# Attention units of one head pair over all batches, first outputs moved inside SBUF, one mask pass for both score banks, and four short decay scans in place of one long one

## The chip, the cores and the metric

The kernel runs on one core of one Trainium2 chip. The metric is the device time of one execution in microseconds (us), lower is better. The engines are called here by the names of the trace: PE (TensorE, matmuls), PEld (its weight loads), DVE (VectorE), ACT (ScalarE), POOL (GpSimd) and SP (SyncE, which issues the DMAs; SPq, ACTq and so on are the instruction queues of the engines). SBUF is the core's working memory with 128 partitions, PSUM the banks that matmuls write, DRAM the device memory.

## The reference, cut to what matters

```python
# attention with decay: q, k, v, alpha are [B=4, H=8, S=768, D=48]
for t in range(S):
    state = alpha[:, :, t, :, None] * state + einsum('bhd,bhe->bhde', k[:, :, t], v[:, :, t])
    y[:, :, t] = einsum('bhd,bhde->bhe', q[:, :, t], state)
x = y.transpose(0, 2, 1, 3).reshape(3072, 384)          # token by (head, d)
# layer 1
h = x @ w_in                                            # 384 -> 2048
g = (a0 + a1*h + a2*h**2 + a3*h**3) / (1 + |b0|*|h| + |b1|*h**2 + 1e-6)
x = g @ w_out                                           # 2048 -> 384
# layer 2
h = x @ w_in2;  out = (h * cos(h)) @ w_out2
```

The attention is computed in chunks. Inside a chunk of 128 steps, p is the running product of alpha; q is multiplied by p and k by 1/p, the scores are a causal matrix product of the two, and the state is carried from chunk to chunk with the last p of the chunk (`pc`).

## The kernel before, in words

The sequence is cut into 6 chunks of 128 steps. A **unit** of the attention is one chunk of one batch: 4 head pairs side by side on the columns (4 x 128 = 512), the two heads of a pair on the partitions. There are 24 units, and unit u stands for chunk u // 4, batch u % 4. The order of the work is written out by hand: a loop over slots n = -3 to 24, in each of which `attention(n)` issues one step for several units at once, and then the fetches and the conversion of the layers' weights. From slot 20 on (`LEAD`) layer 1 begins beside the last four units. After that PE works through layer 1 and layer 2 in blocks of 512 tokens (NF = 16 tiles of 128 hidden columns each), the last blocks with a three-by-three fast product ("threes").

What one regular slot of the attention asks of each engine:

- DVE: `decay` (a 128x4 max, L259, which seeds the first column, and one running product of 512 columns, L260, whose second operand `fresh` is a PSUM bank that holds a floor value everywhere else); `last_decay` (L268); the two steps of the reciprocal (L284, L292); two steps of weight conversion (L75, L76); two of the state's update (L355, L357). In slots 2 to 6 also `y_lo` (L406).
- POOL: q times p (`scale_q`, L303) and k times 1/p (`scale_k`, L298), the low half of a weight (L205), and `mask1`, the causal selection, once for each of the two score banks (L323, tiles hi and lo, 512 columns each).
- ACT: `mask0`, the copy of each score bank out of PSUM (L318, twice), Ln and Exp for 1/p (L275, L276), the output's and the transposed k's copy (L400, L336), and three steps of weight conversion (L70, L71, L195).
- PE: `scores` (L311), the state's part and the scores' part of the output (L376, L386), the transposes (L331) and the update (L343).
- SP: loads of a (the decays), kq and v for later units, one weight tile, and the store of a finished output (`y_store`, L416). Outputs are kept in two buffers in turn, so `y_out` of unit u waits until the store of unit u - 2 has landed.

Layer 1 reads its input x with head features on the partitions and 512 tokens on the columns. The first block's input (chunk 0) is wanted as a high and a low half. Before, the outputs of the first four units go to DRAM as two halves (`y_store`, with `rest=True` for the low one) and come back as 8 loads of rows of 128 floats (`x_pieces`, L1307, slots 8 to 15). The later blocks' inputs are read back by `x_load`, 4 DMAs each (L675). All DMAs go through SP's queue in the order written; a DMA also waits until the one eight before it has landed. An instruction of SP that waits holds up all behind it.

The score banks are the PSUM tiles acc0 and acc1, which the layers use for their sums too. The weight conversion has one PSUM bank (`words_t`) for its intermediate words.

Of the kernel before, what the change touches and what calls it, by code (L numbers as in the profile page):

```python
# [40 lines left out]
def attn_then_two_moe(ctx, tc, kqT, aT, vP, w1i, w1o, ma, mb, w2i, w2o, out):  # L41
# [6 lines left out]
    x0d = dram.tile([2, B, 128 * HP, C], F32, name="x0")  # L48
# [10 lines left out]
    def to_f32(t, r, by=None):  # L59
# [9 lines left out]
        def words():  # L69
# [6 lines left out]
            lambda: nc.vector.scalar_tensor_tensor(ti, hi, -0x80000000, both, ALU.bitwise_and, ALU.bitwise_or),  # L76
# [17 lines left out]
    def temp(tag, dtype=F32, shape=(128, TB)):  # L94

        bufs = {"z": 3, "ah": 2, "g": 4, "hi": 3, "lo": 3}[tag]
        return el.tile(list(shape), dtype, tag=tag, name=tag, bufs=bufs)
# [6 lines left out]
    fresh = bank("r1", (128, HP, C))  # L104
    words_t = bank("b2", (128, TB), I32)[:, :DM]
# [4 lines left out]
    a_t = [a_all[:, i] for i in range(3)]  # L110
# [5 lines left out]
    ws = [[wp.tile([128, 2, DM], F32R, tag=f"w{s}_{i}", name=f"w{s}_{i}") for i in range(NF)] for s in range(2)]  # L116
# [12 lines left out]
    y_rest = xt[0, 0].rearrange("p a b c -> p (a b c)")  # L129
# [3 lines left out]
    MORE = 20  # L133
    slot = [0]
# [25 lines left out]
    def words_bank(w):  # L160

        if slot[0] <= LEAD + 2 and not later[0]:
            return words_t
# [4 lines left out]
    def tick(k, ahead=0):  # L168

        while k and steps and (len(steps) > ahead or fetched[0] == fetched[1]):  # L170
            w, i = steps[0]
            if i == 0:
                t = st_all[:, w_order.index(w) % 4]
                stage[w] = t, to_f32(t, raw64.pop(w), words_bank(w))
# [23 lines left out]
    def w_lo(engs):  # L198
        engs = list(engs)
        while to_lo:  # L200
            (m, s, i), hi = to_lo.pop(0)
# [3 lines left out]
            engs[0].tensor_tensor(out=lo, in0=full, in1=hi.bitcast(F32), op=ALU.subtract)  # L205
            engs.append(engs.pop(0))
# [16 lines left out]
    def load(u, name):  # L223
# [9 lines left out]
        elif u == 0 and name == "a":  # L233
            for cs in (slice(0, HP + HP // 2 * C), slice(HP + HP // 2 * C, HP * (C + 1))):
                nc.sync.dma_start(out=t[:, cs], in_=src[:, cs])
# [17 lines left out]
    def decay(u):  # L253
# [3 lines left out]
        first, rest = a[:, :HP].unsqueeze(2), a[:, HP:].rearrange("p (a b) -> p a b", a=HP)  # L257
        for hs in parts(u):
            nc.vector.tensor_tensor(out=fresh[:, hs, 0:1], in0=first[:, hs], in1=fresh[:, hs, 1:2], op=ALU.max)  # L259
            nc.vector.tensor_tensor_scan(  # L260
                d["p"][:, hs].rearrange("p a b -> p (a b)"), rest[:, hs].rearrange("p a b -> p (a b)"),
                fresh[:, hs].rearrange("p a b -> p (a b)"), 0.0, ALU.mult, ALU.max,
            )

    def last_decay(u):
        d = U[u]
        d["pc"] = in_p.tile([128, HP, 1], F32, tag="pc", name="pc", bufs=6)
        nc.vector.tensor_tensor(out=d["pc"], in0=d["p"][:, :, C - 1:], in1=fresh[:, :, 1:2], op=ALU.max)  # L268
# [36 lines left out]
    def scores(u):  # L305
        d = U[u]
        d["sc"] = [ps_acc.tile([128, HP, C], F32, tag=f"acc{j}", name=f"sc{j}") for j in range(2)]
# [5 lines left out]
    def mask0(u):  # L313
        d = U[u]
        d["s"] = []
        for j, sc in enumerate(d.pop("sc")):
            s = temp(("hi", "lo")[j], shape=(128, HP, C))
            nc.scalar.activation(out=s, in_=sc, func=AF.Copy, scale=-1.0)  # L318
            d["s"].append(s)
# [41 lines left out]
    def y_state(u):  # L361
        c, b = divmod(u, B)
        d = U[u]
        if u == NU - 1:
            d["y"] = ps_acc.tile([128, HP, C], F32, tag="acc0", name="y")
# [25 lines left out]
    def y_out(u):  # L391
        d = U[u]
        if u < NU - B:
            d["yo"] = kept[2 + u % 2]
            if 2 <= u < B:
                d["yo"] = y_rest[:, (2 + u) * TB:(3 + u) * TB].bitcast(F32).rearrange("p (a t) -> p a t", a=HP)
# [1110 lines left out]
```

## Time and profile before

| what | value |
|---|---|
| time, median of 3 runs | 918.09 us (916.93 to 919.14) |
| the profiled execution's own time | 916.58 us |
| its span in the trace | 914.9 us |
| PE busy | 893.7 us, 98% of the span |
| DVE, ACT, POOL busy | 703.8, 695.5, 710.0 us |
| granted TensorE clock | 1.00 in every window that was read |

The times of the rows further down are microseconds from the start of the span of the profiled execution. Its own time is 1.68 us longer than the span, and 1.51 us below the median of the runs.

### The profile page before, as it was taken

The page shows a single profiled execution, that of the slowest core. Times are in us where ns is not written, and L with a number is a line of the kernel's source. Part 1 is how long each engine was busy: PE and PEld are TensorE (multiplying, and loading weights), DVE is VectorE, ACT ScalarE, POOL GpSimd, SP SyncE. Part 2 cuts the span into 40 slices and gives each one's busy share as a digit, 9 for nine tenths or more (in the row PEclk, how much of TensorE's full clock was granted, in tenths as well). Part 3 has the DMA queues.
Part 4 walks back from the last instruction along what each step waited for, and adds up shares of the span by engine and source line. Part 5 has one row for each costly group of instructions (what it writes and reads, how often), then busy time and mean ns, then how long its engine had stood idle before and what let it go on. Part 6 is the DMA issues. An engine that isn't in the chain of part 4 may idle for free.

```text
span 914.9 us, 15676 instructions
## 1 busy us (share of the span) xinstructions
PE 893.7 (98%) x5348; PEld 740.6 (81%) x5348; DVE 703.8 (77%) x1247; ACT 695.5 (76%) x1302; POOL 710.0 (78%) x699
## 2 busy tenths in 40 slices
PE   7899989999999999999999999999999999999997
PEld 6787767888888888888888888878888888888885
DVE  8998789999899989979979968666367554555552
ACT  6998888888879788878778878756577666666653
POOL 7999999989789979879879767758887475655332
PEclk9999999999999999999999999999999999999999
DMA  9999840100234132232165467530243432533432
GB/s 324 388 380 379 331 132 18 31 22 18 69 113 121 44 126 74 78 121 87 41 190 195 153 209 252 196 120 27 69 139 104 155 123 89 171 104 104 139 104 90
DMA packets 67305, 128.83 MB, mean 141 GB/s; under 512 B 6928, under 2 KB 30224, under 8 KB 67216
## 3 DMA queue, kind: packets, MB, share of 16 engines
q1 hardware_dynamic: 67216, 127.74, 41.4%
q8 instruction: 44, 0.72, 0.3%
q14 instruction: 45, 0.37, 0.1%
HBM read 95.21 MB, written 32.51 MB: 140 GB/s over the span
## 4 chain that ended last, share of the span: by engine, by line
PE 86%; ACT 6%; DMA 3%; DVE 3%; issue 2%; POOL 0%; SPq 0%; ACTq 0%; DVEq 0%
PE b L537 28%; PE acc L553 28%; PE acc L1032 15%; PE b L997 6%; PE r L997 5%; DMA x0d<-g 1%; PE b L1176 1%; ACT hi L318 1%; ACT lo L318 1%; ACT r L275 1%; ACT st L70 1%; DMA kq<-kqT 1%; ACT g L336 1%; ACT w L195 1%; DVE p L260 1%
## 5 line engine op out<-in xcount | busy, mean ns | idle before, releaser
L537 PE MATMUL b<-x,w 128*128 128x512 f32 x1143 | 288.2, 396 | 2.5 <-DVE g L606 1.4
L537 PEld LDWEIGHTS b<-x,w 128*128 128x128 f32 x1143 | 214.3, 188 | 55.4 <-DVE g L606 2.0
L553 PE MATMUL acc<-hi,w 128*128 128x512 f32 x738 | 251.5, 395 | 0.0
L588 POOL TENSOR_TENSOR lo<-g,hi 128x512 fp32r<-128x512 f32 x128 | 173.5, 1355 | 70.0 <-ACT hi L583 63.7
L553 PEld LDWEIGHTS acc<-hi,w 128*128 128x128 f32 x738 | 138.7, 188 | 32.9
L1089 POOL TENSOR_TENSOR lo<-g,hi 128x512 fp32r<-128x512 f32 x64 | 83.0, 1297 | 103.6 <-ACT hi L1088 91.6
L553 PE MATMUL acc<-lo,w 128*128 128x512 f32 x369 | 146.2, 396 | 0.0
L583 ACT ACTIVATE hi<-g 128x512 fp32r<-128x512 f32 x128 | 80.6, 630 | 80.7 <-DVE g L619 43.4
L614 POOL TENSOR_TENSOR z<-z,ah 128x512 f32<-128x512 f32 x96 | 127.2, 1325 | 8.0
L1032 PE MATMUL acc<-hi,w_out 128*128 128x512 f32 x384 | 130.4, 396 | 0.0
L615 DVE TENSOR_TENSOR g<-g,b 128x512 f32<-128x512 f32 x96 | 65.3, 680 | 24.0 <-ACT g L612 23.4
L553 PEld LDWEIGHTS acc<-lo,w 128*128 128x128 f32 x369 | 69.4, 188 | 17.0
L1032 PEld LDWEIGHTS acc<-hi,w_out 128*128 128x128 f32 x384 | 68.7, 188 | 9.9
L1032 PE MATMUL acc<-lo,w_out 128*128 128x512 f32 x192 | 76.3, 397 | 0.4 <-POOL lo L1089 0.2
L613 POOL TENSOR_SCALAR z<-ah,cq 128x512 f32<-128x512 f32 x96 | 74.7, 778 | 2.1 <-ACT ah L611 2.1
L612 ACT ACTIVATE g<-b,cq 128x512 f32<-128x512 f32 x96 | 74.5, 776 | 0.0
L619 DVE SCALAR_TENSOR_TENSOR g<-g,cq,r 128x512 f32<-128x512 f32 x96 | 70.8, 738 | 0.1
L606 DVE SCALAR_TENSOR_TENSOR g<-g,cq,b 128x512 f32<-128x512 f32 x96 | 70.7, 736 | 0.0
L623 ACT ACTIVATE r<-z,lnb 128x512 f32<-128x512 f32 x96 | 66.7, 695 | 1.1 <-POOL z L614 1.1
L608 DVE SCALAR_TENSOR_TENSOR r<-z,r 128x512 f32<-128x512 f32 x96 | 65.6, 683 | 0.0
L603 DVE SCALAR_TENSOR_TENSOR z<-z,r 128x512 f32<-128x512 f32 x96 | 64.9, 676 | 0.0
L611 ACT ACTIVATE ah<-b 128x512 f32<-128x512 f32 x96 | 56.4, 587 | 7.5 <-PE b L537 7.3
(192 smaller groups left out, 1814.9 us busy)
## 6 DMA issues: line engine op xcount, KB each, us to landing
w_out<-wd SPq DMA_DIRECT2D x64, 384.0 KB, 3.0
kq<-kqT SPq DMA_DIRECT2D x24, 512.0 KB, 6.5
raw<-w2i SPq DMA_DIRECT2D x16, 384.0 KB, 3.5
w<-wd SPq DMA_DIRECT2D x16, 384.0 KB, 3.0
raw<-w2o SPq DMA_DIRECT2D x16, 384.0 KB, 3.3
wd<-w SPq DMA_DIRECT2D x16, 384.0 KB, 2.5
a<-aT SPq DMA_DIRECT2D x23, 258.0 KB, 5.7
v<-vP SPq DMA_DIRECT2D x24, 192.0 KB, 6.4
```

The source lines that it names most:

```text
L537: nc.tensor.matmul(h, ws[0][f][:, w, ks], x[:, xx, kk, :], start=i == 0, stop=i == 8)
L553: nc.tensor.matmul(acc[k], ws[1][f][:, w, ks], d[g], start=first and i == 0, stop=last and i == 2)
L583: nc.scalar.activation(out=t["hi"], in_=t["g"], func=AF.Copy)
L588: eng.tensor_tensor(out=t["lo"], in0=t["g"], in1=t["hi"].bitcast(F32), op=ALU.subtract)
L606: nc.vector.scalar_tensor_tensor(g, g, cq[:, 3:4], two["h"], ALU.add, ALU.mult)
L612: nc.scalar.activation(out=g, in_=h, func=AF.Identity, scale=cq[:, 5:6], bias=cq[:, 4:5])
L613: nc.gpsimd.tensor_scalar(zz, ah, cq[:, 1:2], cq[:, 0:1], ALU.mult, ALU.add)
L614: nc.gpsimd.tensor_tensor(out=zz, in0=zz, in1=ah, op=ALU.mult)
L619: nc.vector.scalar_tensor_tensor(g, g, cq[:, 2:3], r, ALU.add, ALU.mult)
L997: nc.tensor.matmul(tile[:, half], w[p], x[q], start=start and i == 0, stop=True, skip_group_check=True)
L1032: nc.tensor.matmul(acc[k], item["w"][:, w, ks], item[g], start=first, stop=last)
L1089: nc.gpsimd.tensor_tensor(out=p["lo"], in0=p["g"], in1=p["hi"].bitcast(F32), op=ALU.subtract)
```

## The change

A unit becomes one chunk of one head pair over all four batches: the host lays the inputs out so, and the columns of a unit are 4 batches x 128 steps. The work on the engines for one unit keeps its shape. The input `a` loses its four extra columns (258 KB becomes 256 KB a load). With it:

- The first four units' outputs stay in SBUF (`y_home`, which is the space of the last eight of the layer's first weights) and are moved from there to layer 1's input by 10 DMAs inside SBUF (`y_move`, L437, slots 3 to 6), with both halves in one DMA. The 8 stores and 8 loads of before fall away.
- `x_load` of later blocks makes 10 DMAs of 48, 32 or 16 rows of 2 KB (L690) where 4 DMAs with rows of 512 bytes stood.
- acc0 and acc1 become the halves of one PSUM tile `pair`; `mask0` is one copy of 1024 columns (L328), `mask1` one selection of 1024 columns (L333).
- `decay` is four running products of 128 columns, each of which starts from 1.0 (L272); the floor is one PSUM column, broadcast. There is no max ahead of them.
- The words of the weight conversion go to two banks in turn, and the floor's column is read from the bank that is not in use.

```diff
+    words_t = [bank(tag) for tag in ("b2", "r1")]
+    def floor(shape):
+        t = words_t[1 - lately[0]][:, DM:DM + 1]
+        return (t if len(shape) == 2 else t.unsqueeze(1)).to_broadcast(shape)
+    pair = ps_acc.tile([128, 2, TB], F32, tag="acc01", name="acc01")
+    w_late = wp.tile([128, 2 * B, 2, DM], F32R, tag="w0_8", name="w0_8")
+    y_home = w_late.rearrange("p i a b -> p i (a b)")
...
-        for hs in parts(u):
-            nc.vector.tensor_tensor(out=fresh[:, hs, 0:1], in0=first[:, hs], in1=fresh[:, hs, 1:2], op=ALU.max)
+        for h in range(HP):
             nc.vector.tensor_tensor_scan(
-                d["p"][:, hs].rearrange("p a b -> p (a b)"), rest[:, hs].rearrange("p a b -> p (a b)"),
-                fresh[:, hs].rearrange("p a b -> p (a b)"), 0.0, ALU.mult, ALU.max,
+                d["p"][:, h], a[:, h * C:(h + 1) * C], floor([128, C]), 1.0, ALU.mult, ALU.max
...
-        for j, sc in enumerate(d.pop("sc")):
-            s = temp(("hi", "lo")[j], shape=(128, HP, C))
-            nc.scalar.activation(out=s, in_=sc, func=AF.Copy, scale=-1.0)
+        d["m2"] = temp("hl", shape=(128, 2, TB))
+        nc.scalar.activation(out=d["m2"], in_=pair, func=AF.Copy, scale=-1.0)
...
-        for s in U[u]["s"]:
-            nc.gpsimd.affine_select(
-                s, s, pattern=[[0, HP], [1, C]], compare_op=ALU.is_ge, fill=0.0, base=0, channel_multiplier=-1
-            )
+        s = U[u].pop("m2").rearrange("p j (a t) -> p (j a) t", t=C)
+        nc.gpsimd.affine_select(
+            s, s, pattern=[[0, 2 * HP], [1, C]], compare_op=ALU.is_ge, fill=0.0, base=0, channel_multiplier=-1
+        )
...
+    def y_move(u):
+        for h in (2 * u, 2 * u + 1):
+            for kk, to, of in head_rows(h):
+                nc.sync.dma_start(
+                    out=xt[0, 0][to, :, kk, :].bitcast(F32), in_=y_home[of, 2 * u:2 * u + 2, :TB].bitcast(F32)
+                )
...
+            for h in range(H):
+                for k, to, of in head_rows(h):
+                    if k == kk:
+                        rows = xd[0][blk, h // 2].rearrange("(p b) t -> p (b t)", b=B)
+                        nc.sync.dma_start(out=x[to], in_=rows[of])
...
-            if n >= 8 and x_pieces:
-                x_pieces.pop(0)()
```

The instructions of DVE in a regular slot (p is the running product, a the decays, b and r the two PSUM banks; "waits" names the engine or DMA whose signal the instruction waits for). Before:

```order
L259 TENSOR_TENSOR r_94<-a,r_94 128x4 [waits DMAHW4_49]
L260 SCALAR_TENSOR_TENSOR p<-a,r_94 128x512 [waits DVE_49,Pool_49]
L75 SCALAR_TENSOR_TENSOR b_95<-st,b_95 128x384 [waits Activation_49]
L355 TENSOR_TENSOR u<-s_141,u 128x192 [waits PE_49]
L76 SCALAR_TENSOR_TENSOR st<-spare,b_95 128x384 [waits DMAHW1_49,DVE_49]
```

With the change:

```order
L272 SCALAR_TENSOR_TENSOR p<-a,b_93 128x128 [waits DMAHW6_49,Pool_49]
L272 SCALAR_TENSOR_TENSOR p<-a,b_93 128x128 x3
L73 SCALAR_TENSOR_TENSOR r_94<-st,r_94 128x384 [waits Activation_49]
L365 TENSOR_TENSOR u<-s_134,u 128x192 [waits PE_49]
L74 SCALAR_TENSOR_TENSOR st<-spare,r_94 128x384 [waits DMAHW3_49,DVE_49]
```

The scan waited for the max on its own engine; now the first of four waits for its data and for POOL, and the other three wait for nothing.

The queue of SP where the attention gives way to layer 1 (yo is an output of the last units, x the input of layer 1's second block, raw the next weight tile to be converted; before, L416 is the store and L675 the load, now L432 and L690). Before:

```order
L416 DMA x0d<-yo 128x512 [waits DMAHW4_49,Activation_49]
L675 DMA x<-x0d 128x4x128 [waits DMAHW5_49,DVE_49]
L675 DMA x<-x0d 64x4x128 [waits DMAHW6_49]
L675 DMA x<-x0d 64x4x128 [waits DMAHW7_49]
L675 DMA x<-x0d 128x4x128 [waits DMAHW0_49]
L156 DMA raw<-w1o 128x768 [waits DMAHW1_49,DVE_49]
```

With the change:

```order
L432 DMA x0d<-yo 128x512 [waits DMAHW6_49,Activation_49]
L690 DMA x<-x0d 48x512 [waits DMAHW7_49,DVE_49]
L690 DMA x<-x0d 48x512 [waits DMAHW0_49]
L690 DMA x<-x0d 32x512 [waits DMAHW1_49]
L690 DMA x<-x0d 16x512 [waits DMAHW2_49]
L690 DMA x<-x0d 48x512 [waits DMAHW3_49]
L690 DMA x<-x0d 48x512 [waits DMAHW4_49]
L690 DMA x<-x0d 16x512 [waits DMAHW5_49]
L690 DMA x<-x0d 32x512 [waits DMAHW6_49]
L690 DMA x<-x0d 48x512 [waits DMAHW7_49]
L690 DMA x<-x0d 48x512 [waits DMAHW0_49]
L165 DMA raw<-w1o 128x768 [waits DMAHW1_49,DVE_49]
```

The weight tile's fetch stands behind ten loads instead of four.

## Rows read from the trace of the kernel before

**Rows 1.** The page, part 1: busy us of each engine (share of the span).

```profile
PE 893.7 (98%) x5348; PEld 740.6 (81%) x5348; DVE 703.8 (77%) x1247; ACT 695.5 (76%) x1302; POOL 710.0 (78%) x699
```

**Rows 2.** Busy time by stretch; last columns granted clock, DMA share, GB/s.

```profile
40.00:45.00 5.00, 5.00 (x82) 4.29 (x80) 4.79 (x13) 4.97 (x12) 4.72 (x7) 1.00 1.05 401
...
70.00:75.00 5.00, 4.40 (x68) 3.61 (x68) 4.29 (x11) 4.27 (x10) 4.63 (x6) 1.00 1.06 359
...
115.00:120.00 5.00, 3.87 (x35) 2.88 (x33) 4.51 (x7) 4.97 (x11) 4.92 (x6) 1.00 0.01 3
...
400.00:690.00 290.00, 290.00 (x1325) 236.93 (x1324) 218.12 (x364) 214.24 (x405) 231.85 (x240) 1.00 0.43 142
```

**Rows 3.** Timeline of PE: the scores of units 6, 14 and 20.

```profile
35.70 1.05 PE L311 MATMUL sc<-kq 48*128 48x128 f32 x14
...
70.59 1.16 PE L311 MATMUL sc<-kq 48*128 48x128 f32 x16
...
99.91 1.16 PE L311 MATMUL sc<-kq 48*128 48x128 f32 x16
```

**Rows 4.** Timeline of ACT in one regular slot and the start of the next.

```profile
45.81 0.62 ACT L318 ACTIVATE hi<-sc 128x512 f32<-128x512 f32 x1
46.28 0.63 ACT L318 ACTIVATE lo<-sc 128x512 f32<-128x512 f32 x1
46.76 0.64 ACT L275 ACTIVATE r<-p 128x512 f32<-128x512 f32 x1
...
50.18 0.60 ACT L318 ACTIVATE hi<-sc 128x512 f32<-128x512 f32 x1
```

**Rows 5.** Chain that ended last: start, duration, piece.

```profile
64.73 6.19 DMA x0d<-g
...
75.20 5.70 DMA x0d<-g
...
122.32 4.58 DMA raw<-w1o
```

**Rows 6.** Timeline of POOL: a slot, later waits, and the one selection of 128 columns.

```profile
1.35 0.29 POOL L1277 TENSOR_SCALAR_AFFINE_SELECT ident<-ident 128x128 f32<-128x128 f32 x1
...
44.98 1.27 POOL L303 TENSOR_TENSOR kq<-kq,p 128x512 f32<-128x512 f32 x1
...
48.40 0.64 POOL L323 TENSOR_SCALAR_AFFINE_SELECT hi<-hi 128x512 f32<-128x512 f32 x1
48.98 0.64 POOL L323 TENSOR_SCALAR_AFFINE_SELECT lo<-lo 128x512 f32<-128x512 f32 x1
49.59 1.27 POOL L303 TENSOR_TENSOR kq<-kq,p 128x512 f32<-128x512 f32 x1
...
69.27 1.27 POOL L298 TENSOR_TENSOR kq<-kq,z 128x512 f32<-128x512 f32 x1
...
73.04 1.28 POOL L303 TENSOR_TENSOR kq<-kq,p 128x512 f32<-128x512 f32 x1 [0.37 <-DMA kq<-kqT]
```

**Rows 7.** Timeline of DVE: the first two scans, and a regular slot.

```profile
3.22 0.69 DVE L260 TENSOR_TENSOR_SCAN p<-a,r 128x256 f32<-128x256 f32 x1
...
45.02 0.16 DVE L259 TENSOR_TENSOR r<-a,r 128x4 f32<-128x4 f32 x1
45.28 1.22 DVE L260 TENSOR_TENSOR_SCAN p<-a,r 128x512 f32<-128x512 f32 x1
46.42 0.54 DVE L75 SCALAR_TENSOR_TENSOR b<-st,b 128x384 int32<-128x384 int32 x1
```

**Rows 8.** Timeline of SP's queue at the transition to layer 1.

```profile
113.38 6.36 SPq L416 DMA_DIRECT2D x0d<-yo  x2
119.83 2.38 SPq L675 DMA_DIRECT2D x<-x0d  x4
122.32 0.44 SPq L156 DMA_DIRECT2D raw<-w1o  x1
```

**Rows 9.** The page, part 6: a weight fetch of the same size; KB each, us to landing.

```profile
raw<-w2i SPq DMA_DIRECT2D x16, 384.0 KB, 3.5
```

More of the change, by code (lines that the diff above doesn't have):

```diff
@@ L1 @@
 from contextlib import ExitStack
-from functools import partial
 import numpy as np
@@ L109, in attn_then_two_moe @@
     a_all = const.tile([128, 3, HP * (C + 1)], F32, tag="a", name="a")
-    a_t = [a_all[:, i] for i in range(3)]
+    a_t = [a_all[:, i, :HP * C] for i in range(3)]
     kq_all = const.tile([128, 5, 2, HP, C], F32, tag="kq", name="kq")
@@ L172, in tick @@
             if i == 0:
-                t = st_all[:, w_order.index(w) % 4]
-                stage[w] = t, to_f32(t, raw64.pop(w), words_bank(w))
+                at = w_order.index(w)
+                lately[0] = at % 2 if slot[0] < LEAD else 0
+                words = words_bank(w)
+                t = st_all[:, at % 4]
+                full = words.bitcast(F32) if at in ON_VECTOR and lately[0] and words is not None else t
+                stage[w] = full, to_f32(t, raw64.pop(w), words, full)
             t, ops = stage[w]
@@ L196, in w_hi, with w_lo @@
             to_lo.append((w, hi))
[L198 to L201, printed above, removed]
+    def w_lo(eng, words=False):
+        for item in list(to_lo):
+            (m, s, i), hi = item
+            if words != (stage[m, s, i].space == PS):
+                continue
+            to_lo.remove(item)
             at = early(m, s, i)
@@ L204, in w_lo @@
             full = stage.pop((m, s, i))
[L205 to L206 removed]
+            eng.tensor_tensor(out=lo, in0=full, in1=hi.bitcast(F32), op=ALU.subtract)
             ready.add((m, s, i))
@@ L306, in scores @@
         d = U[u]
-        d["sc"] = [ps_acc.tile([128, HP, C], F32, tag=f"acc{j}", name=f"sc{j}") for j in range(2)]
+        d["sc"] = [pair[:, j].rearrange("p (a t) -> p a t", a=HP) for j in range(2)]
         for hp in range(HP):
@@ L364, in y_state @@
         if u == NU - 1:
-            d["y"] = ps_acc.tile([128, HP, C], F32, tag="acc0", name="y")
+            d["y"] = pair[:, 0].rearrange("p (a t) -> p a t", a=HP)
         elif u > LEAD:
@@ L427, in convert @@
                 turn[:] = [2, 0, 0, 3, 0]
+        if place == 0:
+            w_lo(nc.vector, True)
         if n == LEAD + 2 and place == 4:
@@ L1282, in attn_then_two_moe @@
         warm_up(13)
-        x_pieces = [p for kk in range(NK) for p in x_load(0, 0, kk)]
         for n in range(-3, NU + 1):
@@ L1374, in general @@
                     nc.sync.dma_start(out=rows[:, b], in_=y[:, b])
+            yh = fb.tile([128, HP, B, 2, D], F32, name="yh")
+            nc.sync.dma_start(out=yh.rearrange("p h b j e -> p h (b j e)"), in_=yd)
             for b in range(B):
-                yh = two.tile([128, DM], F32, name="yh")
-                nc.sync.dma_start(out=yh, in_=yd[:, b, :])
                 y = two.tile([128, DM], F32, name="yt")
-                nc.vector.tensor_copy(y.rearrange("p (e a) -> p e a", a=HP), yh.rearrange("p (a e) -> p e a", a=HP))
+                for h in range(H):
+                    nc.vector.tensor_copy(y[:, h * D:(h + 1) * D], yh[:, h // 2, b, h % 2])
                 for kk in range(NK):
```

109 lines of the change are left out of this document (46 added, 63 removed).

## The prediction

> **What bounds the kernel now.** I read the busy times of the page first, then the busy time by stretch, to see where PE loses time at all. PE is busy for 893.7 us of the span's 914.9 [rows 1]. From 400 to 690 us it is busy for all of 290 us, and the clock is 1.00 in every window, so the change can gain only ahead of that, in the attention and in the transition to layer 1; there each us by which the attention ends sooner comes off the end. The windows show three regimes [rows 2]. At 40 to 45 us PE, ACT (4.97 of 5) and DVE (4.79) are all full and the DMA queues too (share 1.05). At 70 to 75 us all four engines have gaps (PE 4.40, ACT 4.27, DVE 4.29, POOL 4.63) while the DMA share stays above 1, at 359 GB/s in place of 401. At 115 to 120 us the DMA queues are empty and PE is at 3.87 behind ACT and DVE.
>
> The pace follows from the starts of the scores on PE, which come once a unit: unit 6 at 35.70 us, unit 14 at 70.59, unit 20 at 99.91 [rows 3]. That is 4.36 us a unit for eight units, then 4.89 for six. ACT shows the 4.36 too: the same copy starts at 45.81 and 50.18, 4.37 apart, with no gap [rows 4].
>
> Why 4.89? The chain of waits has two long pieces of a store's landing, 6.19 us from 64.73 and 5.70 us from 75.20 [rows 5]; each ends at ACT's next output copy, because the outputs have only two buffers. And POOL waits for a load of kq (0.37 us at 73.04) [rows 6]. Both are the DMA queues. A slot there moves 256 (a) + 512 (kq) + 192 (v) + 384 (weight) + 256 (output) KB = 1.64 MB by the code, and before the change one of the 8 returning pieces on top (1.57 MB in all, 0.2 MB each): 1.83 MB, at 359 GB/s 5.1 us, more than a slot. POOL is full up to there as well: its slot takes 49.59 - 44.98 = 4.61 us, against 4.36 of the others, so it loses the head start it began with. At unit 14 its scaled k is done at 69.27 + 1.27 = 70.54, just 0.05 us ahead of PE's scores [rows 3, 6].
>
> **The change, part by part.** *The first outputs inside SBUF.* 8 stores and 8 loads, 3.7 MB of DRAM traffic with 512-byte rows in the loads, give way to 1.57 MB inside SBUF, in slots 3 to 6, a time when DMA has some head start. From slot 8 on a slot asks 1.64 MB, 4.1 us at 401 GB/s and 4.6 us at 359 [rows 2]. I take the higher rate, since the lower one is seen only in stretches that hold the pieces. Then DMA is no longer behind, the stores land in time for the output copies, and the slots from unit 14 on run at the pace of the engines.
>
> *One selection on POOL.* One selection of 512 takes 0.64 us and lets the next start after 0.58 and 0.61; one of 128 takes 0.29 [rows 6]. So a column costs (0.64 - 0.29)/384 = 0.91 ns, the fixed part is 0.18 us, and 1024 columns take some 1.1 us: POOL's slot falls by 0.1 to 0.14 us, to 4.47. That is still longer than the others' 4.35, but POOL starts ahead: its 4.61 us slots used up 8 x 0.25 = 2 us of lead between units 6 and 14. With the masks of 13 units cheaper by 0.135 (1.8 us) it has 1.8 us of lead there, and loses 6 x 0.12 = 0.7 of it up to unit 20. It no longer bounds.
>
> *One copy on ACT.* Two copies take 46.76 - 45.81 = 0.95 us [rows 4]. One of 1024 saves one fixed part, which no row shows by itself. Bounds: nothing, and half of the 0.47 us that one copy takes. I take 0.1, so ACT's slot becomes 4.27. The selection behind it and the scores of the next unit wait for the end of both copies in either version.
>
> *Four scans.* Before: 0.26 us from the max to the scan and 1.14 from the scan to the next instruction, 1.40 in all [rows 7]. A scan of 256 takes 0.69 and one of 512 1.22, so 0.16 is fixed, and one of 128 takes 0.42. Four cost 4 x 0.42 = 1.68 at most. But the instruction behind the scan of 1.22, which does not wait for it, starts after 1.14, that is 0.08 early. The order lists no wait for three of the four; at 0.34 each they cost 1.36, which is 0.04 less than before. I take 0.34, because that row is the same operation on the same tile; both ends stay for the range. [...]
>
> *The slot that results.* PE's own work in a slot, gapless at 40 to 45 us [rows 2], is at most the 4.36 it shows. With DVE at 4.33 and ACT at 4.27 I take 4.35. Units 6 to 20 take 14 x 4.35 = 60.9 us in place of 99.91 - 35.70 = 64.2: **-3.3 us**. The start up to unit 6 (two scans of 256 at 0.69 and two maxes at 0.26, 1.9 us [rows 7], become four short scans, 1.4 to 1.7 us; six cheaper selections) gives **-0.4** (bounds -0.2 to -0.6). Two mask copies in the transition, where ACT is the bound (4.97 of 5 at 115 to 120 us [rows 2]): **-0.2** (bounds 0 to -0.4).
>
> *Ten loads for four.* In the transition SP waits 6.36 us for outputs, then issues the four loads of block 2's x in 2.38 us (0.6 each), then the weight tile whose landing, 4.58 us later, stands on the chain that ended last [rows 5, 8]. Whatever SP does longer ahead of this fetch comes out at the end one for one. Ten loads with few long rows: if an issue costs like the other single ones (0.44 [rows 8]) 4.4 us, +2.0; at 0.6 each 6 us, +3.6; as a lower bound the same 2.4. Against that the tile's landing is queued behind less: 3.5 us for the same size elsewhere [rows 9], 1.1 less than 4.58. I take +2.0 - 1.1 = **+0.9** (bounds -1.1 to +3.6). The same loads in the later blocks and the waits that now join acc0 with acc1 lie beside work of PE that runs without a gap; for small waits at block starts I add **+0.1** (bounds 0 to +0.4).
>
> *Costed at nothing:* the second bank for the words (DVE's second step waits for the first either way), the four fewer columns of a (0.05 MB over the attention), and the moves of slots 3 to 6 (the DMA queues hide them; if they held up kq at all, POOL's lead of 2 us would be the cover).
>
> Sum: -3.3 - 0.4 - 0.2 + 0.9 + 0.1 = -2.9 us. The profiled execution took 916.58, so 913.7; the median of the runs lies 1.51 above it, so **915.2 us**. What a measurement of this kernel can tell from no change is 0.2%, 1.8 us.
>
> **The rivals.** *First, slower: the short scans cost their full time.* If each scan occupies DVE for 0.42 us, its slot is 4.37 - 1.40 + 1.68 = 4.65 and DVE alone sets the pace of all units: 14 x 4.65 = 65.1, +0.9 against now, and +1.3 in the first six units (6 x 0.28, less the start's 0.4); with -0.2, +0.9 and +0.1 the sum is +3.0, 921.1 us. It decides from about 0.38 us a scan on, where the sum is zero. For it speaks that no row shows two scans of the same length in a row; against it the 1.14 behind a scan of 1.22. [...] Chance 0.18.
>
> *Second, same: the ten loads eat the gain.* At 0.6 us each and with the landing no shorter, +3.6 in place of +0.9: -0.2 in all, 917.9 us. For it: 0.6 is what the four take now. Against: those have four times as many rows for their bytes, and single loads take 0.44. Chance 0.12.
>
> *Third, same: DMA goes on setting the pace from unit 14.* If 359 GB/s is what the queues give in that stretch whatever the rows, a slot takes 4.6 us, six slots 27.4 in place of 29.3, and the sum is -1.9 - 0.1 - 0.4 - 0.2 + 1.0 = -1.6, 916.5 us. Against it: 401 GB/s at 40 to 45 us with loads of the same kinds. Chance 0.15.
>
> *Fourth, faster still:* regular slots of 4.30 (if PE's 4.36 holds small waits for DVE and ACT), -4.0, and a weight tile that is not late at all: -4.0 - 0.5 - 0.3 = -4.8, 913.3 us. Chance 0.15.
>
> **How the numbers follow.** My forecast has 0.40; its own range is 913.5 to 917. It and the fourth lie on the faster side of 916.25 but for a share of the first's upper end, the third straddles that bound, the second is the same, the first is slower from 919.9 on, which it reaches at some 0.40 us a scan. That gives faster 0.55, same 0.28, slower 0.17. The range 911.5 to 920.5 takes in all of the middle cases, the fourth with a further 2 us, and the lower half of the first.
>
> **What would show it.** Scores of unit 20 near 96 us, and 4.35 apart from unit 6 on, with no long store on the chain after 60 us: the DMA step is right. The four scans start 0.34 apart (0.42: the first rival). One copy of 1024 near 0.95 and one selection near 1.1 us. The weight tile's fetch at the transition: its issue relative to the last output, and its landing near 3.5 us. PE without gaps from 130 us on. The prediction is wrong if DVE's slot is longer than 4.5, if SP's ten loads take 6 us, or if POOL still waits for kq after unit 14.

## The result: slower by half a per cent

The changed kernel took 922.1 us in the median of 8 runs (920.67 to 924.67), the kernel before, on the same chips, 917.69 (916.38 to 919.14, 8 runs). The ratio is 1.0052, with a 95% interval of 1.0038 to 1.0067. A gain of 2.9 us was forecast (915.2 us, range 911.5 to 920.5). The medians here and below leave out three slow executions, one of the late moves (1244.95 us, at a granted clock of 0.655) and two of the kernel before beside it (942.29 us at 0.898, 2244.21 at 1.00). The profiled execution of the changed kernel has a span of 920.3 us, 5.4 more than before.

The busy times of the engines, which answer to [rows 1]:

```profile
PE 898.4 (98%) x5348; PEld 743.4 (81%) x5348; DVE 699.8 (76%) x1294; ACT 694.5 (75%) x1278; POOL 708.7 (77%) x675
```

DVE, ACT and POOL each do a little less than before; PE is busy for 4.7 us more with the same matmuls. Where the span grew is read from the start of the same instruction in both traces (scores of a unit, then the first matmuls of layer 1 behind the transition):

| what starts | before, us | after, us | later by |
|---|---|---|---|
| scores of unit 6 | 35.70 | 35.95 | 0.25 |
| scores of unit 7 | 40.03 | 40.28 | 0.25 |
| scores of unit 9 | 48.70 | 52.29 | 3.59 |
| scores of unit 20 | 99.91 | 101.62 | 1.71 |
| scores of unit 23 | 118.62 | 119.87 | 1.25 |
| nine matmuls b<-x,w behind PE's gap | 129.82 | 132.23 | 2.41 |
| the matmuls acc behind those nine | 132.03 | 135.98 | 3.95 |
| (whole span) | 914.9 | 920.3 | 5.4 |

So units 7 to 9 lose 3.3 us, units 9 to 20 gain 1.9, the last units up to 23 another 0.5, the transition loses 1.2, the nine matmuls behind it 1.5, and a last 1.5 goes after that.

The scores of units 7, 8 and 9, around the loss, on PE of the changed kernel:

```profile
40.28 1.16 PE L322 MATMUL acc<-kq 48*128 48x128 f32 x16
...
46.10 1.16 PE L322 MATMUL acc<-kq 48*128 48x128 f32 x16 [0.18 <-POOL kq L309]
...
52.29 0.94 PE L322 MATMUL acc<-kq 48*128 48x128 f32 x12 [0.17 <-POOL kq L309]
```

Two units take 5.8 and 6.2 us where [rows 3] have 4.36 on average. PE waits for POOL, and the timeline of POOL in the changed kernel says for what:

```profile
43.54 1.27 POOL L314 TENSOR_TENSOR kq<-kq,p 128x512 f32<-128x512 f32 x1 [2.38 <-DMA kq<-kqT]
...
46.96 1.09 POOL L333 TENSOR_SCALAR_AFFINE_SELECT hl<-hl 128x1024 f32<-128x1024 f32 x1
49.73 1.27 POOL L314 TENSOR_TENSOR kq<-kq,p 128x512 f32<-128x512 f32 x1 [1.69 <-DMA kq<-kqT]
50.96 1.27 POOL L309 TENSOR_TENSOR kq<-kq,z 128x512 f32<-128x512 f32 x1
...
53.14 1.10 POOL L333 TENSOR_SCALAR_AFFINE_SELECT hl<-hl 128x1024 f32<-128x1024 f32 x1
54.20 1.28 POOL L314 TENSOR_TENSOR kq<-kq,p 128x512 f32<-128x512 f32 x1
```

Two loads of kq are 2.38 and 1.69 us late; ACT at the same time waits 3.06 us for a store and DVE 2.00 us for a load of a. All of them come from the DMA queues. The busy time by stretch of the changed kernel (last three columns: granted clock, DMA share, GB/s) shows what happened just ahead of it:

```profile
20.00:30.00 10.00, 8.01 (x118) 6.35 (x114) 9.93 (x30) 9.90 (x20) 9.17 (x10) 1.00 1.04 331
30.00:40.00 10.00, 9.05 (x147) 7.60 (x148) 9.70 (x30) 9.27 (x20) 8.86 (x8) 1.00 0.89 242
40.00:50.00 10.00, 8.43 (x133) 6.99 (x128) 6.55 (x22) 6.91 (x13) 5.93 (x7) 1.00 1.03 342
70.00:75.00 5.00, 4.82 (x78) 3.94 (x75) 4.78 (x14) 4.97 (x11) 5.00 (x6) 1.00 1.06 415
...
130.00:135.00 5.00, 2.77 (x7) 2.18 (x8) 4.64 (x8) 4.61 (x9) 3.55 (x4) 0.75 0.12 43
...
400.00:690.00 290.00, 290.00 (x1317) 236.40 (x1316) 216.26 (x361) 212.74 (x402) 231.62 (x239) 1.00 0.43 141
```

The kernel before in the first two of these stretches:

```profile
20.00:30.00 10.00, 7.35 (x109) 5.86 (x107) 9.72 (x26) 9.92 (x21) 10.00 (x12) 1.00 1.03 397
30.00:40.00 10.00, 9.29 (x152) 7.82 (x152) 9.72 (x26) 9.33 (x21) 10.00 (x12) 1.00 1.04 380
```

From 20 to 40 us, when the ten moves inside SBUF are under way, the queues are nearly always busy but bring only 331 and 242 GB/s, where the kernel before has 397 and 380. From 52 us on the queues are fast again (415 at 70 to 75 us, against 359 before), and POOL, without a gap, sets the pace: 54.20 - 49.73 = 4.47 us a unit. From 400 to 690 us PE is as full as before.

### The profile page after: what moved, and what is told of

It reads as the page before. It is cut to its first block, busy times and chain, and to the rows that moved or that the text cites. A ratio compares the mean times of both kernels' runs of the same rounds, so it can differ in the third digit from the quotient of the medians.

```text
span 920.3 us, 15706 instructions
## 1 busy us (share of the span) xinstructions
PE 898.4 (98%) x5348; PEld 743.4 (81%) x5348; DVE 699.8 (76%) x1294; ACT 694.5 (75%) x1278; POOL 708.7 (77%) x675
## 4 chain that ended last, share of the span: by engine, by line
PE 86%; ACT 6%; DMA 4%; issue 1%; DVE 1%; POOL 1%; SPq 1%; ACTq 0%; DVEq 0%
PE b L562 28%; PE acc L578 28%; PE acc L1046 15%; PE b L1011 6%; PE r L1011 5%; ACT hl L328 1%; DMA raw<-w1i 1%; PE b L1191 1%; DMA v<-vP 1%; ACT r L286 1%; DMA a<-aT 1%; DMA x0d<-g 1%; ACT st L68 1%; ACT w L208 1%; SPq L690 0%
## 5 line engine op out<-in xcount | busy, mean ns | idle before, releaser
L578 PE MATMUL acc<-hl,w 128*128 128x512 f32 x1107 | 278.1, 395 | 0.0
L578 PEld LDWEIGHTS acc<-hl,w 128*128 128x128 f32 x1107 | 208.1, 188 | 50.1 <-ACT kq L593 0.3
L614 POOL TENSOR_TENSOR hl<-g,hl 128x512 fp32r<-128x512 f32 x128 | 173.4, 1355 | 71.7 <-ACT hl L609 68.1
L1104 POOL TENSOR_TENSOR hl<-g,hl 128x512 fp32r<-128x512 f32 x64 | 83.0, 1297 | 104.5 <-ACT hl L1103 104.5
L1046 PE MATMUL acc<-hl,w_out 128*128 128x512 f32 x576 | 153.7, 397 | 0.4 <-POOL hl L1104 0.2
L609 ACT ACTIVATE hl<-g 128x512 fp32r<-128x512 f32 x128 | 80.7, 630 | 77.8 <-DVE g L645 41.6
L1046 PEld LDWEIGHTS acc<-hl,w_out 128*128 128x128 f32 x576 | 100.3, 188 | 18.9 <-POOL hl L1104 2.4
L650 ACT ACTIVATE r<-r 128x512 f32<-128x512 f32 x96 | 55.9, 582 | 3.1
L1088 DVE SCALAR_TENSOR_TENSOR ah<-z,b 128x512 f32<-128x512 int32 x44 | 30.2, 685 | 36.7 <-ACT z L1084 36.7
L220 POOL TENSOR_TENSOR w<-st,w 128x384 fp32r<-128x384 f32 x48 | 50.2, 1048 | 3.5 <-ACT w L208 3.1
```

Of the source, the lines that this page charges most:

```text
L578: nc.tensor.matmul(acc[k], ws[1][f][:, w, ks], d[g], start=first and i == 0, stop=last and i == 2)
L609: nc.scalar.activation(out=t["hi"], in_=t["g"], func=AF.Copy)
L614: eng.tensor_tensor(out=t["lo"], in0=t["g"], in1=t["hi"].bitcast(F32), op=ALU.subtract)
L1046: nc.tensor.matmul(acc[k], item["w"][:, w, ks], item[g], start=first, stop=last)
L1104: nc.gpsimd.tensor_tensor(out=p["lo"], in0=p["g"], in1=p["hi"].bitcast(F32), op=ALU.subtract)
```

## The experiments

Each kernel was timed beside the kernel before on the same chip, and the ratio is to that one. The chips differ from row to row, and the kernel before takes 917.7 to 918.7 us on them, so a difference of less than 1 us between two medians of the table says nothing. The starts of the scores are from one trace of each kernel. Unit 6 starts anywhere from 34.3 to 37.5 us in them, so the last column, from unit 6 to unit 20, is the one to compare.

| kernel | median us | ratio (95% interval) | unit 9 at | unit 20 at | units 6 to 20 |
|---|---|---|---|---|---|
| before | 917.7 to 918.7 | 1 | 48.70 | 99.91 | 64.2 |
| changed | 922.1 | 1.0052 (1.0038 to 1.0067) | 52.29 | 101.62 | 65.7 |
| late moves | 924.02 | 1.0056 (1.0036 to 1.0075) | 50.47 | 102.48 | 65.0 |
| through DRAM | 925.56 | 1.0083 (1.0059 to 1.0106) | 49.29 | 102.40 | 66.1 |
| wide moves | 916.97 | 0.9986 (0.9975 to 0.9997) | 48.76 | 96.35 | 60.6 |
| ten wide | 917.37 | 0.9991 (0.9979 to 1.0002) | 47.86 | 97.56 | 62.8 |
| direct | 919.12 | 1.0009 (0.9998 to 1.0021) | 47.80 | 98.28 | 63.5 |
| two banks | 920.01 | 1.0019 (1.0007 to 1.0032) | 52.76 | 102.70 | 67.9 |
| fetch first | 919.2 | 1.0016 (1.0000 to 1.0032) | 51.16 | 100.46 | 64.3 |
| both | 918.38 | 1.0004 (0.9987 to 1.0021) | 53.24 | 101.61 | 66.4 |
| direct, both | 917.15 | 0.9983 (0.9973 to 0.9993) | 48.89 | 99.21 | 63.3 |
| wide, both | 914.05 | 0.9951 (0.9933 to 0.9968) | 47.93 | 95.88 | 60.9 |
| as others | 914.61 | 0.9957 (0.9945 to 0.9969) | 48.44 | 98.32 | 64.0 |
| before, short | 919.17 | 1.0006 (0.9993 to 1.0020) | 49.41 | 101.35 | 65.1 |

Changed, two banks, fetch first and both have the same ten moves in the same slots, and still their traces show 64.3 to 67.9 us there. One trace of such a kernel is thus good to some 2 us in this stretch; the two with the three wide moves show 60.6 and 60.9.

### Is it the place of the moves, or the path inside SBUF?

Late moves issue one move a slot from slot 8 on, through DRAM sends the same rows by way of DRAM:

```diff
-                nc.sync.dma_start(
-                    out=xt[0, 0][to, :, kk, :].bitcast(F32), in_=y_home[of, 2 * u:2 * u + 2, :TB].bitcast(F32)
-                )
+                moves.append((
+                    xt[0, 0][to, :, kk, :].bitcast(F32), y_home[of, 2 * u:2 * u + 2, :TB].bitcast(F32)
+                ))
...
+            if n >= 8:
+                y_moves(1)
```

> The changed kernel with the same ten moves inside SBUF, but one a slot in slots 8 to 17 in place of two or three a slot in slots 3 to 6. Theory A (the moves come where the loads of kq, a and v are just in time; their place is what costs): the waits of 2.4 and 1.7 us of POOL for kq and of 3.1 us of ACT for a store around 40 to 50 us vanish, the scores of unit 9 start near 49.5 in place of 52.3, those of unit 20 near 97 to 98 in place of 101.6, and the time falls by 3 to 5 us, to 917 to 919. Theory B (each move inside SBUF holds the DMA queues wherever it stands): the waits reappear between 57 and 100 us, spread out, and the time stays within 1 us of 922.

```diff
+        for i in range(2):
+            nc.sync.dma_start(out=x0d[i, u], in_=y_home[:, 2 * u + i, :TB].bitcast(F32))
...
+                moves.append((
+                    xt[0, 0][to, :, kk, :].bitcast(F32), x0d[:, u, of, :].rearrange("i p t -> p i t")
+                ))
```

> The changed kernel with the first four outputs stored to DRAM in both halves (8 stores, slots 3 to 6) and read back by ten loads of 48, 32 or 16 rows of 2 x 2 KB, one a slot in slots 8 to 17: the way of the kernel before with the new rows. If a path inside SBUF is what is slow (theory B), there is no long wait at 40 to 50 us nor later, and the time is 917 to 919, below the run with late moves. If bytes and place decide (theory A), it is as fast as the run with late moves or up to 1 us slower, for its 2.1 MB of additional stores.

Neither gained. With late moves units 7 to 12 start 4.33 us apart, but from unit 14 (72.29) to unit 20 (102.48) a unit takes 5.03 us, and POOL waits for kq seven times, 4.9 us in all. Theory A fell: the loss only moved to where the moves are. Theory B held for the waits, but its reason fell with the second run: by way of DRAM unit 20 starts at 102.40, and POOL waits eight times, 5.9 us. What both have in common with the changed kernel is ten DMAs of 48, 32 or 16 rows. From the late moves an estimate of the price of one, if the queues set the whole slot: 5.03 us, less 1.64 MB at 408 GB/s (the rate of the changed kernel from 80 to 90 us), 4.0 us, leaves 1.0 us of the queues for 157 KB, which at 408 GB/s would take 0.4.

### Rows of one DMA

Wide moves carry the same 1.57 MB in slots 3 to 5 in place of 3 to 6, as three DMAs of 128 rows:

```diff
-        for h in (2 * u, 2 * u + 1):
-            for kk, to, of in head_rows(h):
-                nc.sync.dma_start(
-                    out=xt[0, 0][to, :, kk, :].bitcast(F32), in_=y_home[of, 2 * u:2 * u + 2, :TB].bitcast(F32)
-                )
+        if u < NK:
+            nc.sync.dma_start(out=xt[0, 0][:, :, u, :].bitcast(F32), in_=y_home[:, 2 * u:2 * u + 2, :TB].bitcast(F32))
```

> The changed kernel with the same 1.57 MB moved inside SBUF in slots 3 to 5, but as three DMAs of 128 rows instead of ten of 48, 32 or 16 rows; the rows land in other places, so the first block of the output is not the reference's. Theory (few rows at a time are what holds the DMA queues; such moves cost about 1 us of all queues for 157 KB wherever they stand): the rate stays near 400 GB/s from 20 to 40 us, the waits of POOL for kq at 40 to 50 us shrink from 4.1 us to below 1, the scores of unit 9 start near 49.5 to 50 in place of 52.3, and the time falls by 3 to 4 us, to 918 to 919. Rival (the bytes, or the path inside SBUF): the waits stay above 3 us and the time within 1 us of 922.

```profile
30.00:40.00 10.00, 9.21 (x152) 7.77 (x152) 9.70 (x31) 9.28 (x20) 10.00 (x10) 1.00 1.04 401
40.00:50.00 10.00, 10.00 (x161) 8.45 (x158) 9.69 (x33) 9.94 (x20) 10.00 (x10) 1.00 1.01 386
```

These are the two stretches of the wide moves that answer to 242 and 342 GB/s above: 401 and 386, with POOL full. The share alone does not explain it: per full share the changed kernel's stretch from 30 to 40 us has 242 / 0.89 = 272 GB/s, this one 401 / 1.04 = 386, so the queues were slower there and not only idle. No wait of POOL for kq is left behind 10 us. Unit 20 starts at 96.35, units 6 to 20 take 96.35 - 35.78 = 60.6 us. The time falls by 5.1 us by the medians and 6.1 by the ratios, more than expected.

Three DMAs instead of ten could also have done it, since each waits for the one eight before it, or the time that SP's queue is at them (8.0 us for the ten moves, 1.9 for the three). Ten wide ones tell that apart (308 columns each, 7.2 us of SP's queue):

> The changed kernel with ten moves inside SBUF in the same slots as its own (two, three, three, two), each of 128 rows of 308 columns, the same 1.57 MB in all (in other places, so the first block of the output is not the reference's). It tells the number of DMAs from the number of rows. Theory (few rows at a time hold the queues): as the three wide moves, no wait of POOL for kq above 1 us, units 4.33 apart, scores of unit 20 at 96 to 97, 916 to 918. Rival (ten DMAs use up the eight places in flight and SP's time): the waits of 4 us at 40 to 50 us come back, scores of unit 20 at 100 to 102, 920.5 to 923.

917.37 us, unit 20 at 97.56: nearly all of the gain, with ten DMAs. Its stretch from 30 to 40 us:

```profile
30.00:40.00 10.00, 9.29 (x152) 7.85 (x148) 9.66 (x32) 9.27 (x20) 8.76 (x8) 1.00 0.97 337
```

But the expectation of no wait above 1 us failed: POOL waits 2.4 us in all, 1.8 the longest, the queues bring 337 GB/s, and from unit 7 to unit 20 it takes 58.5 us, against 61.3 for the changed kernel and 56.2 with three moves. So of these 5.1 us, 2.9 go with the number of rows and 2.2 with the number of DMAs or the shorter rows (1.2 KB instead of 2), which no run separates. The split is that of single traces: the four with ten moves of few rows have 60.0 to 63.6 us there, all above 58.5, so the rows' part is between 1.5 and 5.1 us. No run here measures one DMA of few rows alone, and two loads of 64 rows in the run as others below left POOL with a single wait for kq of 0.3 us, so what it is in the few rows that costs stays open. What these runs show is the rate of all queues together, 242 GB/s at a share of 0.89 with the ten moves of few rows in flight, and loads of kq that come 2.38 and 1.69 us too late behind it.

### The two other losses

Two banks separates the joint PSUM tile again (one selection stays), fetch first puts the weight tile's fetch ahead of the ten loads:

```diff
-        d["sc"] = [pair[:, j].rearrange("p (a t) -> p a t", a=HP) for j in range(2)]
+        d["sc"] = [ps_acc.tile([128, HP, C], F32, tag=f"acc{j}", name=f"sc{j}") for j in range(2)]
...
-        nc.scalar.activation(out=d["m2"], in_=pair, func=AF.Copy, scale=-1.0)
+        for s, sc in zip(d["s"], d.pop("sc")):
+            nc.scalar.activation(out=s, in_=sc, func=AF.Copy, scale=-1.0)
...
-                    acc[k] = pair[:, k] if k < 2 else ps_acc.tile([128, TB], F32, tag="acc2", name="acc2")
+                    acc[k] = ps_acc.tile([128, TB], F32, tag=f"acc{k}", name=f"acc{k}")
```

> The changed kernel with two separate PSUM tiles acc0 and acc1 again, copied by two instructions of 512 columns; the one selection of 1024 columns on POOL stays. Theory: the joint tile makes the second sum of a new block wait for a copy of the first, at four places of the three-by-three stage, 0.24 us each; these waits go and the time falls by 0.7 to 1.1 us, to about 921.1. Rival: PE waits for something else at the same places and the time stays within 0.3 us. The attention stays as it is in both, since POOL sets its pace.

The waits of the changed kernel from 640 us on hold the row that the expectation rests on (us in total, times, longest), and in the run with two banks the row is gone:

```profile
PEld acc L1046 <- ACT g L601: 0.7, 4, 0.2
```

Four weight loads of PE wait for ACT's copy of the other sum. In the changed kernel PE's matmuls of the last stage fall behind by 0.24 to 0.27 us at four places, from 3.99 to 5.01 us behind the kernel before. With two banks they stay where they are, 5.2 us behind from 640 us to the end. So the joint tile costs 1.0 us, as expected. The median fell by 2.1 us, and the same edit gave 0.8 on top of fetch first; the interval of each run reaches some 1.2 us to either side. What the first gives beyond 1.0 stays open, and its trace doesn't show it: that execution took 922.21 us. Its attention was longer than the changed kernel's, and the clock fell in it as well:

```profile
40.00:50.00 10.00, 8.21 (x94) 6.90 (x93) 6.85 (x21) 7.24 (x15) 5.61 (x6) 0.75 1.03 355
```

```diff
+                if late:
+                    for kk in range(NK):
+                        x_load(*nxt, kk)
```

(behind `w_fetch`, in place of the same loop ahead of it.)

> The changed kernel with the ten loads of the second block's input issued behind the weight tile's fetch in the transition in place of ahead of it. Theory: the fetch is issued 4.6 us earlier, the weight tile no longer ends last, PE's gap of 2.5 us at 129.7 shrinks below 1.4 and the granted clock stays at 1.00 after it (now nine matmuls take 3.9 us there in place of 2.4): 2 to 4 us less, 918 to 920. Rival: the tile isn't what PE waits for, or the late loads of x hold up the next fetch, and the time stays within 0.5 us of 922.

919.2 us, 2.9 less, as expected. In its trace the span is 4.0 us shorter than the changed kernel's; 1.4 of that lie between units 6 and 20, where the code is the same, and are not the edit's. The timeline of SP's queue at the transition, of the changed kernel:

```profile
121.02 4.57 SPq L690 DMA_DIRECT2D x<-x0d  x10
125.69 0.37 SPq L165 DMA_DIRECT2D raw<-w1o  x1
```

The chain that ended last has the landing of that weight tile, in the changed kernel:

```profile
125.69 3.64 DMA raw<-w1o
```

The timeline of PE there, of the kernel before:

```profile
129.82 2.37 PE L537 MATMUL b<-x,w 128*128 128x512 f32 x9 [1.36 <-DVE g L606]
```

Of the changed kernel:

```profile
132.23 3.91 PE L562 MATMUL b<-x,w 128*128 128x512 f32 x9 [2.52 <-DVE g L632]
138.07 2.27 PE L562 MATMUL b<-x,w 128*128 128x512 f32 x9
```

And with the fetch first:

```profile
129.49 2.37 PE L562 MATMUL b<-x,w 128*128 128x512 f32 x9 [0.93 <-DVE g L632]
131.69 2.26 PE L578 MATMUL acc<-hl,w 128*128 128x512 f32 x9
```

The gap falls from 2.52 to 0.93 us, the nine matmuls behind it take 2.37 us in place of 3.91, and the granted clock stays at 1.00 there (0.75 in 130 to 135 us of the changed kernel).

Both joins the edits of these two runs.

> The changed kernel with two separate PSUM tiles for the scores (as in the run with two banks) and the weight tile's fetch ahead of the ten loads (as in the run that fetches first). The two touch different places, so the gains add: 922.1 - 2.1 - 2.9 = 917.1, 916 to 918. If one of the two gained by a wait that the other takes away too, 918 to 920.

918.38: the lower end of the second case, less than the sum of the two. In its trace both edits do what they did alone: the gap is 0.94 us, and PE falls behind no further from 640 us on. But its attention takes 66.4 us against 64.3 with fetch first, with the clock at 0.83 from 40 to 60 us. How long the waits behind the ten moves get differs from trace to trace (POOL's for kq are 3.9 to 7.4 us in all in the four with the same moves), and that covers up gains of 1 us.

### Kernels that could win

Direct writes three pairs' outputs to where layer 1 reads them and fills the gaps of 16 rows from the fourth; later blocks come back in one DMA of 128 rows of 6 KB:

```diff
-                d["yo"] = y_home[:, 2 * u, :TB].bitcast(F32).rearrange("p (a t) -> p a t", a=HP)
+                d["yo"] = first_x(u, 0).bitcast(F32).rearrange("p (a t) -> p a t", a=HP)
...
+        if u == NK:
+            for j in range(2):
+                for g in range(NK):
+                    nc.sync.dma_start(
+                        out=xt[0, 0][64 * j + D:64 * j + 64, :, g, :].bitcast(F32),
+                        in_=y_home[64 * j + g:64 * j + D:NK, 0:2, :TB].bitcast(F32)
+                    )
```

> The changed kernel with another order of layer 1's input rows: the outputs of the first three head pairs are written straight to where layer 1 reads them, and the fourth pair's 96 rows fill the 16-row gaps beside each head (the host orders the weight's rows alike). Of the 1.57 MB of moves 0.39 MB is left (six DMAs of 16 rows in slot 6), later blocks are read back by one DMA of 128 rows of 6 KB in place of ten. Theory: the waits for kq at 40 to 50 us go, POOL keeps its lead, the scores of unit 20 start at 96 to 98 in place of 101.6, the weight tile at the transition is issued 0.5 us behind the outputs, PE's gap there stays below 1.5 us and the clock at 1.00: 914 to 917. Rival: six moves of 16 rows hold the queues as the ten did, and the time stays above 918.

919.12: unit 20 at 98.28, between theory and rival. Six moves of 16 rows, 64 KB each, still bring the queues to 267 GB/s at 30 to 40 us, but at a share of 0.72: here the queues have gaps. SP issues no load from 31 to 40 us: it waits 3.1 us for ACT ahead of a store and is then at these six for 5 us:

```profile
34.80 5.08 SPq L441 DMA_DIRECT2D x<-w  x6
```

POOL waits for kq four times, 3.2 us in all. Even so PE is 2.4 us ahead of the kernel before behind the transition (127.41 against 129.82). It loses most of that later, where layer 1 turns to its next block:

```profile
233.41 2.36 PE L567 MATMUL b<-x,w 128*128 128x512 f32 x9 [0.68 <-DVE g L637]
240.66 2.36 PE L583 MATMUL acc<-hl,w 128*128 128x512 f32 x9 [0.69 <-ACT kq L598]
```

The waits from 225 to 245 us have ACT waiting for that block's input:

```profile
ACT x L696 <- DMA x<-x0d: 5.6, 1, 5.6
```

At 241 us PE is 0.5 us ahead; the four waits of the joint tile put it 0.5 behind, and the end of the span adds 1.0. That ACT's wait is what reaches PE is read from this order of events, and no run takes it apart.

Direct, both adds the two edits of above to it:

> The same order of rows, with the two separate PSUM tiles and the fetch first. The waits of 0.24 us at four places of the three-by-three stage go: 1 to 2 us less than the run before it, 913 to 915, below both kernels. The fetch's place should bring nothing here, since one load stands ahead of it in place of ten.

917.15, 2.0 less than direct and below both kernels by its interval, but 2 above the upper end of the expectation. Its trace shows two of the same losses: 254 GB/s at a share of 0.68 from 30 to 40 us, and ACT's wait for the next block's input, 6.0 us, behind which PE loses 1.0 at 235 us.

Wide, both adds them to the three wide moves:

> The three wide moves (rows in other places, so the first block of the output is not the reference's) together with the two separate PSUM tiles and the fetch first. With wide moves alone 916.97: PE still had a gap of 2.7 us at the transition and the four waits of 0.24 us. Theory: the gap falls to some 1.4 us (-1.3) and the waits go (-1.0): 914 to 915.5. If the parts are one and the same gain: 916 to 917.

914.05, 2.9 less than wide moves: the gains of rows, banks and fetch add up here. PE's gap at the transition is 0.94 us in place of 2.69, and from 640 us on PE loses nothing.

As others keeps the two edits, and sends the first four outputs the way of all others, in rows that lie four apart in DRAM. Every block comes back in four loads, and the first is split into its high and low half in SBUF:

```diff
+        to = x_rows(c).rearrange("(p u) t -> p u t", u=HP)[:, b]
+        nc.sync.dma_start(out=to, in_=U[u]["yo"].rearrange("p a t -> p (a t)"))
...
+            for p, row in {0: [(slice(0, 128), 0)], 1: [(slice(0, 64), 128), (slice(64, 128), 256)],
+                           2: [(slice(0, 128), 320)]}[kk]:
+                nc.sync.dma_start(out=x[p], in_=x_rows(blk)[row:row + p.stop - p.start])
```

> The first four outputs treated like all others: one store of 128 rows each (strided rows in DRAM), read back like the later blocks by four loads of 128, 64, 64 and 128 rows of 2 KB (the host orders the weight's rows alike), and split in SBUF into high and low by three copies of ACT and three subtractions of DVE in slots 12 to 17 in place of the four of slots 2 to 6; two separate PSUM tiles and the fetch first stay. 1.84 MB in rows of 2 KB, 64 or 128 at a time, 4.6 us of the queues at 400 GB/s against the 3.9 of the wide moves. Theory: as fast as the wide moves, units 4.33 apart, scores of unit 20 at 96 to 97.5, and 913.5 to 916 us, with the reference's output; below both kernels. Rival: loads of 64 rows hold the queues as those of 48 do, the kq waits come back after unit 12, and it is 917 or more.

914.61 us, ratio 0.9957 (0.9945 to 0.9969): 0.4% below the kernel before, and faster than both kernels by more than the intervals, with the layout of head pairs, rows of 2 KB, and 64 or 128 of them to a DMA. Its unit 20 starts at 98.32, later than expected: three slots take 5 us, those ahead of the scores of units 14, 16 and 18, in which DVE has a subtraction of the split; PE waits for DVE there three times, 1.9 us in all. With 64.0 us from unit 6 to unit 20 its attention is no faster than before; its trace, of an execution of 916.46 us, gains in the first units (unit 6 at 34.30) and at the transition (gap 0.93).

The last one goes back to the kernel before and takes over the short scans and the one selection alone:

```diff
-            nc.vector.tensor_tensor(out=fresh[:, hs, 0:1], in0=first[:, hs], in1=fresh[:, hs, 1:2], op=ALU.max)
...
+                d["p"][:, h], a[:, HP + h * C:HP + (h + 1) * C], fresh[:, h], 1.0, ALU.mult, ALU.max
...
+        s = U[u].pop("m2").rearrange("p j (a t) -> p (j a) t", t=C)
```

> The kernel before with two parts of the change alone: four scans of 128 columns from 1.0 without the max, and one selection of 1024 columns on POOL (two PSUM tiles and two copies as before); layout, stores, pieces and loads as before. Theory (the DMA queues set the pace of the attention from unit 14 on, so engine time saved there comes back as waits): units 6 to 13 some 0.03 us faster each, the six slots after it as slow as before, 0.3 to 1 us in all, 917 to 918. Rival (the saved time of POOL and DVE counts in every slot): 914.5 to 916.

919.17, no gain: the theory's case in the time, and a bit worse than it said. Units 6 to 14 do not become faster as it said: they take 35.8 us against 34.9, with a wait of POOL for kq of 1.99 us. POOL waits for kq four times, 3.8 us in all, where the kernel before waits 1.1; unit 20 starts at 101.35.

## Why the prediction was wrong

**The step that failed** is the one "costed at nothing": the moves of slots 3 to 6, "the DMA queues hide them". The prediction gave those slots "some head start" of DMA without a row for it; the kernel before has a share of 1.03 and 1.04 from 20 to 40 us, when the moves run, and [rows 2] 1.05 at 40 to 45, so there was no cover. It priced the moves by their bytes (1.57 MB against 3.7), while the runs show that the rows of a DMA count: by the estimate above some 1.0 us of the queues for 157 KB in few rows, 0.4 by bytes. In place of -3.3 from unit 6 on the trace shows +3.3 in two units and -1.9 in the eleven after them.

**POOL's lead.** "POOL starts ahead", "it no longer bounds" was right as long as nothing stopped POOL: with wide moves units stay 4.33 apart though POOL's own slot takes 4.47. In the changed kernel POOL waited 4.1 us for kq, its lead was gone, and its 4.48 set the pace of units 9 to 20. The prediction named POOL's lead as cover, but never worked out what follows once it is used up. Its signs of being wrong missed this: SP's ten loads took 4.57 us and not 6, a unit behind unit 9 takes 4.48, under 4.5, and POOL no longer waits for kq there. That the time lies near the first rival's 921.1 us is chance, since the cause that it named did not occur.

**The third rival's rate** (359 GB/s whatever the rows) is refuted: without the pieces the queues bring 415 GB/s from 70 to 75 us in the changed kernel and 408 from 80 to 90. So it was right to tie the low rate to the pieces and wrong to expect nothing of the kind from the new rows.

**Right:** the slot that results. Forecast 60.9 us for units 6 to 20 with DMA out of the way; the wide moves show 60.6. That is one of two traces with wide moves; the other shows 60.9. No row shows the 4.33 us for DVE's slot that goes into this sum (the 4.37 of [rows 4], less 1.40, plus 1.36); in the changed kernel a round of DVE in which the timeline has no wait, from its scans at 66.29 us to those at 70.61, takes 4.32. The four scans take less than I took, in the changed kernel:

```profile
48.50 1.35 DVE L272 TENSOR_TENSOR_SCAN p<-a,r 128x128 f32<-128x128 f32 x4 [2.00 <-DMA a<-aT]
49.77 0.54 DVE L73 SCALAR_TENSOR_TENSOR b<-st,b 128x384 int32<-128x384 int32 x1
```

From the first scan to the next instruction 1.27 us, 0.32 a scan (taken: 0.34; [rows 7] have 1.40 for the max and the long scan), while one scan by itself lasts 0.39: the four are done after 1.35, not after 1.56, so these scans start before the one ahead of them has ended. The first rival fell with it. The selection takes 1.09 (estimated 1.1). The one copy takes 1.01 to 1.04 and the next instruction starts 0.90 later, against 0.95 for two [rows 4]: 0.05 saved, half of the 0.1 taken.

**Ten loads for four:** 4.57 us against 2.38 [rows 8], +2.2 (taken +2.0); the landing 3.64 against 4.58 [rows 5], -0.9 (taken -1.1). Together +1.25, and the trace shows +1.2 there (taken +0.9). Not foreseen: PE's gap grew from 1.36 to 2.52 us, the clock fell behind it (0.75 from 130 to 135 us), and the nine matmuls took another 1.5. That last part is this execution's: the clock does not fall behind every such gap (last section).

**Joint banks:** taken as +0.1 (bounds 0 to 0.4) with the reason that the waits lie beside work of PE without a gap; measured +1.0 in the trace, four waits that PE does not make up. Another 0.5 us lies behind the start of PE's last matmul, 7.0 us from the end against 6.5 before; its cause is open.

Sum of the trace: +0.3 + 3.3 - 1.9 - 0.5 + 1.2 + 1.5 + 1.0 + 0.5 = 5.4 us. The medians differ by 4.4.

## What to carry to other kernels

Where the windows show a DMA share near 1, as here, do not cost an added transfer at nothing: its price is the time it takes from the queues, which here was more than its bytes say (1.0 us against 0.4 by the estimate from the late moves), so measure it by the rate of the stretch that holds it. Here moves of 128 rows in place of 48, 32 and 16 made the median 5.1 us shorter with three of them and 4.7 with ten; if a layout leaves 48 rows, change the layout (here the order of the weight's rows) rather than issue more small DMAs. And when an engine's lead is what hides a longer slot, work out what the pace is after one stall has used the lead up. Before a loss is read off one trace, compare traces of kernels that share the stretch: here they differ by more than the gains at issue.

## What was not expected of the hardware

With few rows in some DMAs the whole set of queues was slower: 242 GB/s at a share of 0.89 from 30 to 40 us while moves of 48, 32 and 16 rows are in flight, two or three a slot, and 334 to 366 from 50 to 90 us with one a slot (late moves); 401 from 30 to 40 us with three moves of 128 rows, 337 with ten. The source made no difference that shows: unit 20 starts at 102.48 with the late moves from SBUF, at 102.40 through DRAM. And a gap of PE cost more than its length in three traces out of six. These six have a gap of 2.5 to 2.9 us at the transition. Behind 2.52 us (changed), 2.62 (two banks) and 2.90 (late moves) the clock fell, to 0.75 from 130 to 135 us in the first and 0.83 from 130 to 140 in the others, and the nine next matmuls took 3.91 us; behind 2.69 (wide moves), 2.81 (ten wide) and 2.8 (through DRAM) it stayed at 1.00 from 130 to 140 us, and in the first two they took 2.36 and 2.37, as they do behind gaps of 0.93 and 0.94. Late moves and wide moves:

```profile
134.93 3.91 PE L569 MATMUL b<-x,w 128*128 128x512 f32 x9 [2.90 <-DVE g L639]
```

```profile
127.46 2.36 PE L559 MATMUL b<-x,w 128*128 128x512 f32 x9 [2.69 <-DVE g L629]
```

The gap's length does not decide here. What does is open.
